# Bucket codes in one instruction per unit, spread by four transfers; a third query buffer; a token copy that is held back

## The chip, the cores and the metric

The kernel runs on one core of a Trainium2 chip. The time is that of the whole launch on the device, in microseconds (us). TensorE (PE) multiplies matrices into PSUM, VectorE (DVE), ScalarE (ACT) and GpSimd (POOL) work on tiles, and SyncE (SP) issues nearly all transfers. Each engine runs its own list of instructions in order, so one that waits holds up all that stand behind it.

## What is computed

The reference, cut to its core: attention in which a query sees only the keys of its own hash bucket, a feed-forward layer, and a layer with eight experts of which each token uses two.

```python
q_bits = (einsum('bhsd,dk->bhsk', q, proj) > 0)      # 6 bits; the same for k
mask = q_bucket[:, :, :, None] == k_bucket[:, :, None, :]
scores = where(mask, scale * q @ k.T, -1e9)
x = softmax(scores) @ v                              # batch 2, heads 8, 768 tokens, head 64
h = x @ w_in; x = (h * sigmoid(1.702 * h)) @ w_out   # 1536 tokens, 512 -> 2048 -> 512
top2 of noisy gate logits; out[t] += w * (relu(x[t] @ w1[e]) @ w2[e])   # 8 experts, 512 -> 1024 -> 512
```

## The kernel before

The attention runs in 96 steps, g = 0 to 95: a step is one head and 128 queries against all 768 keys. Sixteen steps make a chunk (256 queries, 8 heads); there are three chunks for each of the two batches. In a step PE multiplies queries by keys (`qk`, L227), DVE copies the scores out of PSUM and takes their maximum (`rowmax`, L239), ACT takes the exponential (L248), and the result is split in two halves of 16 bits, by ACT (L287) and by DVE (L294 or L296), and transposed by a DMA (`e_lo`, L300). PE then multiplies by the values (`pv`, L341). Chunk by chunk, some steps behind, the feed-forward layer runs in between (L433, L444), its result goes to the tile `xr`, and the router (`route`) picks two experts per token and scatters the rows to `slots` in DRAM (L658, issued by POOL). The expert layer (L772, L803) follows when all is scattered.

Queries and keys come in units. A query unit (24 of them) holds two heads of 256 queries, a key unit (16) one head of 768 keys. A unit is loaded (`load`, L124 or L128), split into 16-bit halves on ACT, DVE and POOL into a tile `qsa` or `ks` (`stack`), transposed by a DMA into `qt` or `kt` (`turn`, L160), one half of it copied once more by a DMA (`again`, L164), and projected by PE (`buckets`, L173). The projection of a unit is cut in four strips that lie in the PSUM tile `pb` at partitions 0, 32, 64 and 96, twelve rows each: six bits with both signs. `codes` (L181) compares each strip with zero and writes the twelve rows of codes, for that quarter of the tokens, into partitions 64 to 75 of `qt` or `kt`. They are extra rows of the contraction in `qk` (76 rows in its second half), where unequal bits add a penalty that no exponential survives. So `qk` of a step needs the codes of its query unit and its key units. `pb` has one buffer, which the router's small products use too.

Up to step 99 a scheduler decides the order of instructions when the kernel is built, from the order of the code, the dependencies and its own estimates; so any edit may move other work. From step 100 on the order is that of the code. The weights of the feed-forward layer, 64-bit floats, are decoded by DVE (L401, L404, L407) during the first two chunks.

The last two words of a row of `xr` hold the token's number: L612 copies it on DVE. It depends on nothing but a free buffer of `xr`, of which there are two.

Of the kernel before, what the change touches and what calls it, by code (L numbers as in the profile page):

```python
# [8 lines left out]
F16 = mybir.dt.float16  # L9
I32 = mybir.dt.int32  # L10
# [4 lines left out]
OP = mybir.AluOpType  # L15
# [3 lines left out]
DM = H * D  # L19
# [13 lines left out]
CT = 2  # L33
NCH = NT // CT
CQ = CT * 128
NBITS = 6
BIG = 65504.0
# [26 lines left out]
def fused(ctx: ExitStack, tc: tile.TileContext, q, k, v, proj, w_in, w_out, w_gate, w_noise, noise,  # L64
# [16 lines left out]
                            channel_multiplier=1)  # L81
    ident32 = consts.tile([128, 128], F32)
    nc.vector.tensor_copy(ident32, ident)
    pr = {nm: consts.tile([128, 3, 2 * NBITS], F16, name=f"p{nm}") for nm in "qk"}
    thr = consts.tile([128, 2], F32)
    for j in range(4):
        nc.gpsimd.iota(thr[j * 32:j * 32 + 32, 0:1], pattern=[[1, 1]], base=-NBITS, channel_multiplier=1,
# [4 lines left out]
    def proj_parts():  # L92
        p32 = rt.tile([128, NBITS], F32, name="p32", tag="zc", bufs=1)
        nc.sync.dma_start(p32[:64], proj)
        nc.sync.dma_start(p32[64:], proj)

        p3 = rt.tile([128, 3, NBITS], F16, name="p3", tag="z", bufs=1)
        nc.vector.tensor_scalar(p3[:, 0], p32, GP, GP, op0=OP.add, op1=OP.subtract)
        nc.vector.tensor_tensor(p32, p32, p3[:, 0], op=OP.subtract)
        nc.vector.tensor_copy(p3[:, 1], p32)  # L100
        nc.vector.tensor_tensor(p32, p32, p3[:, 1], op=OP.subtract)
        for nm, a0 in (("q", 0), ("k", 64)):
            w = pr[nm]
            h, l = slice(a0, a0 + 64), slice(64 - a0, 128 - a0)
            nc.vector.memset(w[l, 0], 0.0)
            for j in range(2):
                c, sg = slice(j * NBITS, (j + 1) * NBITS), SH if j == (nm == "k") else -SH
                nc.vector.tensor_scalar(w[h, 0:2, c], p3[h, 0:2], sg, 0.0, op0=OP.mult, op1=OP.add)
                nc.vector.tensor_scalar(w[h, 2, c], p32[h], sg, 0.0, op0=OP.mult, op1=OP.add)
                nc.vector.tensor_scalar(w[l, 1:3, c], p3[l, 0:2], sg, 0.0, op0=OP.mult, op1=OP.add)  # L110
# [2 lines left out]
    NU = B * NCH * 4 * HP  # L113


    raw, rows, kts, qts, vts, bks = {}, {}, {}, {}, {}, {}
    FL = "p h c d -> p (h c) d"


# [12 lines left out]
    def stack(nm, b, u):  # L132
        x = raw.pop((nm, b, u)).rearrange(FL)
        nh, n = (2, CT) if nm == "q" else (1, NT)
        if nm == "q":
            sa = att.tile([128, nh, n, 128], F16, name="qsa")
        else:
            sa = moe.tile([128, nh, n, 128], F16, name="ks", tag="wraw" if b else "gt", bufs=PARAM["NW"] if b else 4)
        rows[nm, b, u] = sa
        h0 = 0 if nm == "q" else 64  # L140
        hi, lo = (sa[:, :, :, c:c + 64].rearrange(FL) for c in (h0, 64 - h0))
        nc.scalar.activation(x, x, AF.Copy, scale=SH)
        eng = nc.gpsimd if PARAM["HE"](nm, b) == "P" else nc.vector
        eng.tensor_scalar(hi, x, GX, GX, op0=OP.add, op1=OP.subtract)
        nc.gpsimd.tensor_tensor(lo, x, hi, op=OP.subtract)

    def turn(nm, b, u):
        sa = rows.pop((nm, b, u))
        hp, i = u
        if nm == "q":  # L150
            xt = att.tile([128, 2, 2, CT, 128], F16, name="qt", bufs=3)
            qts[b, hp, i] = xt
        elif i == 0:
            xt = att.tile([128, 2, 2, NT, 128], F16, name="kt", bufs=4)
            kts[b, hp] = xt
        else:
            xt = kts[b, hp]
        dst = (xt if nm == "q" else xt[:, :, i:i + 1]).rearrange("p s h c t -> p s (h c) t")
        rows[nm, b, u] = dst
        nc.sync.dma_start_transpose(dst[:, 0], sa.rearrange("p h c d -> p (h c d)"))  # L160
# [5 lines left out]
    def buckets(nm, b, u):  # L166
        xt = rows[nm, b, u][:, 0].rearrange("p c t -> p (c t)")
        n = xt.shape[1] // 4
        pb = psr.tile([128, NT * 32], F32, name="pb", bufs=1)
        bks[nm, b, u] = pb  # L170
        for s in range(3):
            for j in range(4):
                nc.tensor.matmul(pb[j * 32:j * 32 + 2 * NBITS, :n], pr[nm][:, s], xt[:, j * n:j * n + n],  # L173
                                 start=(s == 0), stop=(s == 2))

    def codes(nm, b, u):
        xt, pb = rows.pop((nm, b, u))[64:KB, 1].rearrange("p c t -> p (c t)"), bks.pop((nm, b, u))
        n, sg = xt.shape[1] // 4, int(nm == "k")
        for j in range(4):
            sl = slice(j * 32, j * 32 + 2 * NBITS)  # L180
            nc.vector.tensor_scalar(xt[:, j * n:j * n + n], pb[sl, :n], thr[sl, sg:sg + 1], -BIG if sg else BIG,  # L181
                                    op0=OP.is_gt, op1=OP.mult)
            yield

    FU = PARAM["FU"]
    vfs = {}
# [351 lines left out]
    rst = {}  # L538
# [6 lines left out]
    def route(ci):  # L545
# [56 lines left out]
        for c in range(2):  # L602
# [2 lines left out]
            yield  # L605
        nc.vector.tensor_tensor(mk[:, ci], oh[:, :, 0], oh[:, :, 1], op=OP.add)
        yield
        nc.vector.tensor_tensor(cum[:, 1], cum[:, 0], mk[:, ci, 0], op=OP.add)
        yield

        me = mst[ci, "xr"][:, :, 2 * DM:].bitcast(F32)
        nc.vector.tensor_copy(mst[ci, "xr"][:, :, 2 * DM:2 * DM + 2].bitcast(I32),  # L612
                              tok[:, b, cc * CT:(cc + 1) * CT, None])
        yield
        nc.vector.tensor_copy(me[:, :, 1:2], ef[:, :, 0:1])
        yield
# [213 lines left out]
    def at(g, f, *a):  # L830
        todo.setdefault(g, []).append((f, a))
# [4 lines left out]
    def soon(g, f, *a):  # L836
        first.setdefault(g, []).append((f, a))
# [22 lines left out]
    def stacks(g, nm, b, u):  # L860
        oh = PARAM["OH"]
        at(g - 2, load, nm, b, u)
        at(g, stack, nm, b, u)
        soon(g + 1, turn, nm, b, u)
        start(g + PARAM['BK'], again, nm, b, u)
        start(g + PARAM['BK'], buckets, nm, b, u)
        at(g + oh, codes, nm, b, u)

    for b in range(B):
        for hp in range(HP):  # L870
# [70 lines left out]
    g_lo = min(todo)  # L941
    for g in range(g_lo, G1 + 1):
        if g == max(PARAM["GM"], g_lo):
            order.enter_context(tc.manual_schedule(engines={
                mybir.EngineType.PE, mybir.EngineType.DVE, mybir.EngineType.Activation,
                mybir.EngineType.Pool, mybir.EngineType.SP}))
        if g == NU + 3:
            att_ctx.close()
            m2 = ctx.enter_context(tc.tile_pool(name="m2", bufs=2))
        prev = steps.get(g - 1, [])  # L950
        if 0 <= g + 2 < NU:
            qk(g + 2)
        for f, a in early.pop(g, []):
            f(*a)
        for x in prev:
            moe_act(*x)
        if 0 <= g + 1 < NU:
            rowmax(g + 1)
            expo(g + 1)
            e_hi(g + 1)  # L960
        for f, a in first.pop(g, []):
            f(*a)
        for x in prev:
            moe_dve(*x)
        if 0 <= g < FU:
            e_turn(g)
            e_copy(g)
        elif FU <= g < NU:
            e_lo(g)
        for x in steps.get(g, []):  # L970
            moe_pe(*x)
        for x in prev:
            moe_split(*x)
        by_turns(todo.pop(g, []))
# [159 lines left out]
```

## Time and profile before

| what | value |
| --- | --- |
| median of 3 runs | 830.18 us (829.44 to 830.46) |
| the profiled execution, whole / span of its instructions | 828.85 / 827.0 us |
| busy: PE, DVE, ACT, POOL | 720.8, 545.6, 442.0, 273.8 us |
| mean granted clock of TensorE | 0.953 of full speed |
| L181, all 160 instructions | 59.98 us on DVE |

The page of the profile gives busy times and the costliest groups over the whole span. Since the stages have different limits, the views by stretch say more: the first chunk ends at about 94 us, the weights are decoded by about 200 us, the second batch begins at about 258 us, and from about 530 us on only the experts run.

### The profile page before, as it was taken

How to read it: one execution, taken by the hardware profiler on the slowest of the kernel's cores; microseconds unless marked ns; L12 is line 12 of the kernel's file. 1: busy time of each engine (PE TensorE's matmuls, PEld its weight loads, DVE VectorE, ACT ScalarE, POOL GpSimd, SP SyncE). 2: the span in 40 equal slices, each digit the busy share in tenths (PEclk: the TensorE clock that was granted, in tenths of full speed). 3: DMA queues.
4: the chain of work that ended last, by engine and by line, in shares of the span. 5: the costliest groups of instructions: out<-in, count | busy, mean ns of one | idle time of the engine just before them, and what ended most of it. 6: DMA issues, size and time to landing. Idle time of an engine off the chain costs nothing.

```text
span 827.0 us, 14864 instructions
## 1 busy us (share of the span) xinstructions
PE 720.8 (87%) x5494; PEld 431.2 (52%) x5495; DVE 545.6 (66%) x1279; ACT 442.0 (53%) x875; POOL 273.8 (33%) x302
## 2 busy tenths in 40 slices
PE   3767787878889788979999999896999999999994
PEld 1444355434654466547557658365545545555452
DVE  8998999988888679667867824563526435354220
ACT  3788676665676566557557715333524435344220
POOL 5446366634456123404222223221120311302112
PEclk9897699998999899999999999998999999999998
DMA  8985586999999996776587550657768768677313
GB/s 206 232 233 149 159 201 151 287 262 225 165 195 201 188 218 119 151 128 106 105 170 116 109 185 14 198 174 201 176 179 235 151 176 185 148 202 156 75 17 44
DMA packets 245340, 136.30 MB, mean 165 GB/s; under 512 B 200016, under 2 KB 221072, under 8 KB 245264
## 3 DMA queue, kind: packets, MB, share of 16 engines
q1 hardware_dynamic: 239248, 122.16, 62.6%
q0 software_dynamic: 6016, 13.16, 8.6%
q8 instruction: 44, 0.72, 0.4%
q14 instruction: 32, 0.26, 0.1%
HBM read 61.48 MB, written 23.20 MB: 102 GB/s over the span
## 4 chain that ended last, share of the span: by engine, by line
PE 46%; DVE 21%; DMA 12%; issue 8%; ACT 5%; POOL 4%; SPq 2%; POOLq 0%; DVEq 0%; ACTq 0%
PE ph L772 15%; PE py L803 14%; PE h L433 6%; PE px L444 5%; DVE e L239 4%; DVE er L296 4%; DMA slots<-xr,si 3%; PE s L227 2%; DMA et<-er 2%; ACT er L287 2%; POOL slots L658 2%; DVE wraw L407 2%; DVE wf L404 2%; DVE qt L181 2%; DMA k<-in_k_dram 2%
## 5 line engine op out<-in xcount | busy, mean ns | idle before, releaser
L772 PE MATMUL ph<-xg,ew 128*128 128x400 f16 (+2 forms) x864 | 136.3, 321 | 10.8 <-DMA xg<-slots 9.9
L444 PE MATMUL px<-wo,gt 128*128 128x512 f16 x576 | 139.1, 392 | 6.9 <-ACT wo L418 4.6
L433 PE MATMUL h<-xt,wi 128*128 128x256 f16 x1152 | 137.2, 275 | 7.3 <-DVE xr L467 3.9
L716 DVE SCALAR_TENSOR_TENSOR ew<-w,ew 128x1024 f16<-128x1024 f32 x64 | 77.9, 1225 | 86.6 <-ACT ew L715 86.6
L433 PEld LDWEIGHTS <-wi 128*128 128x128 f16 x1152 | 111.3, 98 | 28.9 <-issue 10.8
L803 PE MATMUL py<-ew,ht 128*128 128x512 f16 x576 | 125.8, 379 | 0.0
L820 POOL DMA_INDIRECT out_dram<-yo,ti x32 | 50.1, 1564 | 211.2 <-ACT yo L813 201.8
L772 PEld LDWEIGHTS <-ew 128*128 128x128 f16 x864 | 83.4, 101 | 62.1 <-issue 8.1
L227 PE MATMUL s<-kt,qt 76*128 76x256 f16 (+3 forms) x384 | 87.5, 353 | 27.5 <-DVE e L239 24.6
L478 POOL TENSOR_TENSOR gt<-th,gt 128x512 f16<-128x512 f32 x48 | 61.7, 1286 | 113.9 <-ACT gt L477 112.8
L444 PEld LDWEIGHTS <-gt 128*128 128x128 f16 x576 | 56.2, 100 | 75.5 <-issue 17.5
L239 DVE TENSOR_SCALAR_CACHE_REDUCE e<-s 128x768 f32<-128x768 f32 x96 | 90.9, 951 | 5.3 <-PE pt L266 3.9
L296 DVE SCALAR_TENSOR_TENSOR er<-e,mx,er 128x768 f16<-128x768 f32 x68 | 73.5, 1084 | 28.1 <-ACT er L287 27.3
L803 PEld LDWEIGHTS <-ht 128*128 128x128 f16 x576 | 56.2, 98 | 67.1
L248 ACT ACTIVATE e<-e,mx 128x768 f32<-128x768 f32 x96 | 89.3, 930 | 1.8
L287 ACT ACTIVATE er<-e,mx 128x768 f16<-128x768 f32 x68 | 63.1, 931 | 29.2 <-DMA et<-er 16.2
L782 ACT ACTIVATE ht<-ph 128x400 f16<-128x400 f32 (+2 forms) x72 | 33.6, 467 | 69.2 <-PE ph L772 68.9
L715 ACT ACTIVATE ew<-w 128x1024 f16<-128x1024 f32 x64 | 66.4, 1049 | 6.4 <-DMA w<-in_moe_w_dram 6.3
L227 PEld LDWEIGHTS <-qt 76*128 76x128 f16 (+1 forms) x384 | 36.6, 103 | 60.5 <-issue 30.0
L813 ACT ACTIVATE yo<-py,wv 128x512 f32<-128x512 f32 x24 | 16.5, 687 | 87.8 <-PE py L803 51.0
L783 DVE SCALAR_TENSOR_TENSOR ht<-ph,ht 128x400 f16<-128x400 f32 (+2 forms) x72 | 37.5, 524 | 33.9 <-ACT ht L782 33.8
L247 ACT ACTIVATE mx<-mx 128x1 f32<-128x1 f32 x96 | 18.9, 197 | 64.1 <-DVE e L239 63.8
(182 smaller groups left out, 923.9 us busy)
## 6 DMA issues: line engine op xcount, KB each, us to landing
w<-in_moe_w_dram SPq DMA_DIRECT2D x64, 512.0 KB, 4.9
wraw<-in_moe_w_in_dram SPq DMA_DIRECT2D x16, 512.0 KB, 5.3
wraw<-in_moe_w_out_dram SPq DMA_DIRECT2D x16, 512.0 KB, 4.8
slots<-blank SPq DMA_DIRECT2D x6, 1032.0 KB
v<-in_v_dram SPq DMA_DIRECT2D x24, 192.0 KB, 3.0
out_dram<-zeros SPq DMA_DIRECT2D x13, 256.0 KB, 3.4
k<-in_k_dram SPq DMA_DIRECT2D x16, 192.0 KB, 4.4
q<-in_q_dram SPq DMA_DIRECT2D x24, 128.0 KB, 2.9
```

The source lines that it names most:

```text
L227: nc.tensor.matmul(ps[:, n0 * 128:n1 * 128], qt[:kr, s, h, t, :], kt[:kr, s, h, n0:n1, :].rearrange("p c t -> p (c t)"), start=(s == 0), s ...
L239: nc.vector.tensor_scalar(e32, st[g]["ps"][:, :S], -FAR, -TOP, op0=OP.max, op1=OP.max, accum_out=mx[:, 0:1])
L248: nc.scalar.activation(e32, e32, AF.Exp, scale=SS, bias=st[g]["mx"][:, 1:2], accum_out=sms[b, cc, hp][:, 2 * h + t:2 * h + t + 1] if g < N ...
L287: nc.scalar.activation(er[:, 0], st[g]["e"], AF.Copy, scale=r)
L296: nc.vector.scalar_tensor_tensor(er[:, 1], d["e"], d["mx"][:, 3:4], er[:, 0], op0=OP.mult, op1=OP.subtract)
L433: nc.tensor.matmul(ph[:, a, :], wi[ws][:, d, f0:f0 + 128], xt[:, d, xs, :], start=(d == 0 and ws == 0 and xs == 0), stop=(d == HP - 1 and ...
L444: nc.tensor.matmul(px, gts[ci, f // 2][:, gs, f % 2, t * 128:t * 128 + 128], wo[ws][:, f, :], start=(f == 0 and gs == 0 and ws == 0), stop ...
L478: nc.gpsimd.tensor_tensor(gt[:, 1], th, gt[:, 0], op=OP.subtract)
L715: nc.scalar.activation(hi, x, AF.Copy, scale=SW1 if j == 0 else SW2)
L716: nc.vector.scalar_tensor_tensor(lo, x, SW1 if j == 0 else SW2, hi, op0=OP.mult, op1=OP.subtract)
L772: nc.tensor.matmul(ph[:, :c1 - c0], w[:, ws, d * FE + f * 128:d * FE + f * 128 + 128], xg[e, p][:, xs * HP + d, :], start=(d == 0 and ws = ...
L803: nc.tensor.matmul(py, ht[:, f, hs, t * 128:t * 128 + 128], w[:, ws, f * DM:(f + 1) * DM], start=(i == 0), stop=(i == n - 1))
```

## The change

`pr`, the weights of the projection, get 32 columns instead of 12, zeros in the other 20, so that the four strips fill all 128 partitions of `pb`. `codes` compares all of them in one DVE instruction and writes into the unit's `qsa` or `ks` tile, which has been transposed by then. A new step, `spread`, at the start of the next step, moves the four strips to their rows of `qt` or `kt` by four transfers of SP. The `qsa` or `ks` tile is held until these have read it, and `qsa` gets three buffers instead of two. L612 (L617 after) is tied to stand behind the running sum of `route` (`cum`) in DVE's list, as long as the scheduler orders.

```diff
-    pr = {nm: consts.tile([128, 3, 2 * NBITS], F16, name=f"p{nm}") for nm in "qk"}
+    pr = {nm: consts.tile([128, 3, 32], F16, name=f"p{nm}") for nm in "qk"}
...
-            nc.vector.memset(w[l, 0], 0.0)
+            nc.vector.memset(w, 0.0)
...
-            sa = att.tile([128, nh, n, 128], F16, name="qsa")
+            sa = att.tile([128, nh, n, 128], F16, name="qsa", bufs=3)
...
-                nc.tensor.matmul(pb[j * 32:j * 32 + 2 * NBITS, :n], pr[nm][:, s], xt[:, j * n:j * n + n],
+                nc.tensor.matmul(pb[j * 32:j * 32 + 32, :n], pr[nm][:, s], xt[:, j * n:j * n + n],
...
     def codes(nm, b, u):
-        xt, pb = rows.pop((nm, b, u))[64:KB, 1].rearrange("p c t -> p (c t)"), bks.pop((nm, b, u))
+        xt, pb = rows[nm, b, u][64:KB, 1].rearrange("p c t -> p (c t)"), bks.pop((nm, b, u))
         n, sg = xt.shape[1] // 4, int(nm == "k")
+        cd = sas.pop((nm, b, u)).rearrange("p h c d -> p (h c d)")
+        nc.vector.tensor_scalar(cd[:, :n], pb[:, :n], thr[:, sg:sg + 1], -BIG if sg else BIG, op0=OP.is_gt, op1=OP.mult)
+        bks[nm, b, u] = cd
+
+    def spread(nm, b, u):
+        xt, cd = rows.pop((nm, b, u))[64:KB, 1].rearrange("p c t -> p (c t)"), bks.pop((nm, b, u))
+        n = xt.shape[1] // 4
         for j in range(4):
-            sl = slice(j * 32, j * 32 + 2 * NBITS)
-            nc.vector.tensor_scalar(xt[:, j * n:j * n + n], pb[sl, :n], thr[sl, sg:sg + 1], -BIG if sg else BIG,
-                                    op0=OP.is_gt, op1=OP.mult)
-            yield
+            nc.sync.dma_start(xt[:, j * n:j * n + n], cd[j * 32:j * 32 + 2 * NBITS, :n])
...
-        nc.vector.tensor_tensor(cum[:, 1], cum[:, 0], mk[:, ci, 0], op=OP.add)
+        behind = nc.vector.tensor_tensor(cum[:, 1], cum[:, 0], mk[:, ci, 0], op=OP.add)
...
-        nc.vector.tensor_copy(mst[ci, "xr"][:, :, 2 * DM:2 * DM + 2].bitcast(I32),
-                              tok[:, b, cc * CT:(cc + 1) * CT, None])
+        with ExitStack() if rst.get("set") else tc.issue_after(behind.ins):
+            nc.vector.tensor_copy(mst[ci, "xr"][:, :, 2 * DM:2 * DM + 2].bitcast(I32),
+                                  tok[:, b, cc * CT:(cc + 1) * CT, None])
...
         at(g + oh, codes, nm, b, u)
+        soon(g + oh + 1, spread, nm, b, u)
```

What this does to the lists of instructions shows at three places. The first is SP's list at the start of the program (`ks_155` and `qsa_159` are the first key and query unit; `kt`, `qt` their transposed tiles). Before:

```order
L164 DMA kt_163<-kt_163 64x768
L164 DMA qt_165<-qt_165 64x512
L160 DMA_TRANSPOSE kt_163<-ks_211 128x6x128
L390 DMA wraw_225<-in_moe_w_in_dram 128x1024
L124 DMA q32_231<-in_q_dram 128x2x128
L160 DMA_TRANSPOSE kt_233<-ks_227 128x6x128
L164 DMA kt_163<-kt_163 64x768
```

and after:

```order
L164 DMA kt_163<-kt_163 64x768
L164 DMA qt_165<-qt_165 64x512
L187 DMA kt_163<-ks_155 12x192 x4
L187 DMA qt_165<-qsa_159 12x128 x4
L160 DMA_TRANSPOSE kt_163<-ks_213 128x6x128
L394 DMA wraw_227<-in_moe_w_in_dram 128x1024
L124 DMA q32_233<-in_q_dram 128x2x128
L160 DMA_TRANSPOSE kt_235<-ks_229 128x6x128
L164 DMA kt_163<-kt_163 64x768
```

Eight transfers of codes now stand ahead of the next key unit's transposition, and they wait for DVE. From here to the first transposition of a softmax (L300 before, L304 after) SP has 91 transfers before and 133 after: 56 for codes, and 14 others fewer (loads that now come later).

The second place is DVE's list where the copy of the token numbers stands in the second batch's first chunk (`xr_4372` is the third chunk's tile, `er` a step's low half, `xr_2178` the first chunk's). Before:

```order
L467 SCALAR_TENSOR_TENSOR xr_3242<-px_2998,xr_3242 128x512
L296 SCALAR_TENSOR_TENSOR er_3204<-e32_3198,mx_3197,er_3204 128x768
L252 TENSOR_SCALAR mx_3244<-mx_3244 128x1
L239 TENSOR_SCALAR e32_3296,mx_3295<-s_3237 128x768
L253 RECIPROCAL mx_3244<-mx_3244 128x1
L612 COPY xr_4372<-tok_107 128x2
L296 SCALAR_TENSOR_TENSOR er_3251<-e32_3245,mx_3244,er_3251 128x768
```

and the first such copy of the changed kernel (its first chunk; in the kernel before this one stood among the first ten instructions of the program):

```order
L610 TENSOR_TENSOR mk_122<-oh_2923 128x16
L180 TENSOR_SCALAR ks_2650<-pb_2857,thr_87 128x192
L635 RECIPROCAL xr_2178<-d1_2930 128x2
L612 TENSOR_TENSOR cum_123<-cum_123,mk_122 128x8
L617 COPY xr_2178<-tok_107 128x2
L637 TENSOR_TENSOR xr_2178<-xr_2178,d1_2930 128x2
```

The copy has moved from a place some chunks ahead of its own chunk's routing to one inside it.

The third place is SP's list where the second batch's first key units are prepared, between the transpositions of softmax steps. Before:

```order
L164 DMA kt_2929<-kt_2929 64x768
L300 DMA_TRANSPOSE et_2687<-er_2593 128x12x128
L160 DMA_TRANSPOSE qt_2859<-qsa_2814 128x4x128
L160 DMA_TRANSPOSE kt_3057<-ks_3013 128x6x128
L164 DMA qt_2859<-qt_2859 64x512
L300 DMA_TRANSPOSE et_2687<-er_2681 128x12x128
```

and after:

```order
L304 DMA_TRANSPOSE et_2707<-er_2613 128x12x128
L128 DMA k32_2738<-in_k_dram 128x384
L187 DMA kt_2560<-ks_2513 12x192 x4
L187 DMA qt_2562<-qsa_2519 12x128 x4
L304 DMA_TRANSPOSE et_2707<-er_2701 128x12x128
```

Between the two transpositions of a pair of steps stand transfers of codes, which wait for DVE and for nothing else.

## Rows read from the trace of the kernel before

**Rows 1.** Busy us of each engine by stretch of the span, with granted clock and DMA share.
```profile
core 0: us, PE busy (x) PEld busy (x) DVE busy (x) ACT busy (x) POOL busy (x), PEclk, DMA share, GB/s
0.00:94.00 94.00, 57.43 (x443) 32.23 (x444) 83.46 (x198) 63.80 (x151) 48.85 (x86) 0.87 0.78 199
94.00:201.00 107.00, 84.59 (x617) 49.25 (x618) 101.31 (x175) 71.06 (x142) 59.51 (x46) 0.90 0.88 223
201.00:336.00 135.00, 117.79 (x1081) 77.91 (x1081) 111.22 (x296) 87.51 (x194) 53.50 (x49) 0.95 0.91 177
...
365.00:530.00 165.00, 159.94 (x1342) 107.67 (x1340) 112.10 (x309) 97.28 (x196) 46.34 (x44) 1.00 0.60 126
530.00:827.00 297.00, 275.42 (x1859) 151.13 (x1857) 119.83 (x257) 109.03 (x167) 58.62 (x73) 0.97 0.61 151
```

**Rows 2.** L239 by the same stretches: DVE busy, and two instructions for each step.
```profile
0.00:94.00 94.00, 15.25 (x32) 0.87 0.78 199
94.00:201.00 107.00, 19.11 (x40) 0.90 0.88 223
201.00:336.00 135.00, 26.92 (x56) 0.95 0.91 177
```

**Rows 3.** Chain of work that ended last, 336 to 365 us, shares by line.
```profile
by line: DMA slots<-xr,si 28.3%; DMA qt<-qsa 14.8%; issue 13.7%; POOL slots L658 12.2%; DVE er L296 9.6%; DMA q<-in_q_dram 7.2%; DVE e L239 3.8%; POOL qsa L144 3.7%; ACT e L248 3.2%; POOL qsa L145 2.7%; ACT q L142 1.4%; DVE ps__4236 L638 1.
```

**Rows 4.** DVE around L612, in order of time; in brackets the idle time before.
```profile
272.49 0.17 DVE L612 COPY xr<-tok 128x2 int32<-128x2 int32 x1 [6.02 <-DMA slots<-xr,si]
...
351.57 0.17 DVE L612 COPY xr<-tok 128x2 int32<-128x2 int32 x1 [5.91 <-DMA slots<-xr,si]
```

**Rows 5.** PE at the same two places.
```profile
269.78 0.63 PE L341 MATMUL pv<-et,vt 128*64 128x256 f16 x8
275.60 0.66 PE L173 MATMUL pb<-kt,pk 128*12 128x192 f16 x12 [5.19 <-DVE kt L181]
...
355.36 0.81 PE L227 MATMUL s<-kt,qt 128*128 128x512 f16 x4 [3.38 <-DVE e L239]
```

**Rows 6.** L181 over the whole span: duration least, median, most, first and last start.
```profile
L181 DVE TENSOR_SCALAR qt<-pb,thr x96: 342/346/359, 14.6 to 447.5; 12x128 f16<-12x128 f32 x96
L181 DVE TENSOR_SCALAR kt<-pb,thr x64: 407/414/425, 10.9 to 301.2; 12x192 f16<-12x192 f32 x64
```

**Rows 7.** L181 by stretch: DVE busy and instructions, four to a unit.
```profile
0.00:94.00 94.00, 23.03 (x60) 0.87 0.78 199
94.00:201.00 107.00, 5.57 (x16) 0.90 0.88 223
201.00:336.00 135.00, 23.02 (x60) 0.95 0.91 177
```

**Rows 8.** Issue time on SP of small transfers (the four of L739) and of transpositions.
```profile
L739 SPq DMA_DIRECT2D mt<-slots x32: 408/418/482, 563.7 to 762.7; - x32
...
L300 SPq DMA_TRANSPOSE et<-er x80: 1275/1488/6345, 100.0 to 476.2; - x80
```

**Rows 9.** SP's own waits, 0 to 94 us: first and last of 18 (total, times, longest).
```profile
SPq L128 <- POOL vt L209: 7.9, 7, 2.8
...
SPq L128 <- ACT mx L247: 0.2, 1, 0.2
```

**Rows 10.** SP's own waits, 201 to 336 us: first and last of 22.
```profile
SPq L300 <- DVE mx L253: 8.1, 5, 4.2
...
SPq L128 <- POOL vt L209: 0.5, 1, 0.5
```

**Rows 11.** Transfers by line: size, median us from issue to landing.
```profile
kt<-kt SPq DMA_DIRECT2D x16, 96.0 KB, 3.5
...
mt<-slots SPq DMA_DIRECT2D x32, 0.2 KB, 1.8
```

**Rows 12.** What PE and its weight loads waited for, whole span: total, times, longest.
```profile
PE pb L173 <- DVE kt L181: 11.0, 6, 5.2
...
PEld L227 <- DVE qt L181: 4.2, 7, 2.1
```

## What I predicted, before the changed kernel had run

> **What bounds the kernel now.** I read the table by stretch first [rows 1], because the kernel has three different limits. Up to 94 us DVE is busy for 83.5 of 94 us, and from 94 to 201 us for 101.3 of 107: these 201 us hold 36 steps [rows 2] and DVE sets their pace. From 201 to 336 us it is busy for 111.2 of 135 while PE has 117.8, and the transfer engines are at 0.91: nothing is full, and what ends there is a chain of waits. From 365 to 530 us PE has 159.9 of 165, and from 530 us on 275.4 of 297; there nothing that DVE or SP gains can be seen. So an edit pays only by bringing the point at about 365 us forward, where PE has become the limit, and it can pay at most what PE idles before that.
>
> The second view was the chain of waits from 336 to 365 us [rows 3]: 28.3% of it are the scatter transfers to `slots` and another 12.2% POOL issuing them. That is odd, since nobody reads `slots` before the experts. The DVE timeline tells why [rows 4]: twice L612, a copy of a few words, waits 6.02 and 5.91 us for the scatter, because the scheduler put it ahead of time, where its buffer of `xr` is still being read. All of DVE's list stands behind it, and PE runs dry in turn: 5.19 us the first time, 3.38 us the second [rows 5].
>
> Third, SP: its own waits add up to 41.0 us in 0 to 94 (18 rows) and 48.5 us in 201 to 336 (22 rows) [rows 9, 10]. So it issues for about 53 of 94 and 86 of 135 us.
>
> **The change part by part.**
>
> *The held copy (a).* It stands behind its own chunk's sum now, long after the old buffer's scatter. Both stalls should go. DVE gets 11.9 us back [rows 4], but the end only moves by what PE lost, 5.19 + 3.38 = 8.6 us [rows 5]. Ends: 0, if another wait stands at the same place (the next late thing is `er`'s transposition, which SP issues), and 12. I take -8.6, since PE is the limit right behind it.
>
> *Fewer instructions on DVE.* A key unit takes 4 x 0.414 us now and one such instruction after, a query unit 4 x 0.346 [rows 6]: the length is set by the columns, which stay, so I take the same 0.414 and 0.346 for 128 partitions. Saved are 1.24 and 1.04 us a unit, 16 x 1.24 + 24 x 1.04 = 44.8 us in all. By stretch [rows 7]: 15 units (8 keys, 7 queries) in 0 to 94 us, 17.2 us; 4 query units in 94 to 201, 4.2 us; 15 units again in 201 to 336, 17.2 us; the rest lies where PE is the limit and is worth 0.
>
> *Four transfers for it, on SP.* The nearest rows are the four small transfers that the expert stage issues in a row, 0.418 us each [rows 8]; 1.7 us a unit. In 0 to 94 us that is 56 x 0.42 = 23.5 us, less 14 loads that now come later (at about the same 0.42, 5.9 us): 53 + 17.6 = 71 of 94 us. In 201 to 336 it is 60 x 0.42 = 25 us: 86 + 25 = 111 of 135. So SP goes from 56% to 75% and from 64% to 83% at the old pace, and would be at 90% if the pace rose by a tenth. Behind a transfer of codes, which waits for DVE, stand loads and the transpositions of softmax steps (1.49 us each [rows 8]), and behind those POOL, PE and the next units. So the gain of each stretch is cut:
>
> - (b) 0 to 94 us: of 17.2 us I take -3. The first units' transpositions stand behind eight transfers of codes (8 x 0.42 = 3.4 us later, and so on for each unit), so the first steps come later and DVE decodes weights meanwhile; that work is not lost, which is why I expect a small gain and not a loss. Ends -12 (SP never late) and +8 (half of the 17.6 us shows).
> - (c) 94 to 201 us: DVE at 95%, SP with few units; -3.5 of 4.2. Ends -6 (also what was decoded ahead) and 0.
> - (d) 201 to 336 us: neither engine is full. -1; ends -10 and +12 (half of the 25 us).
>
> *The way from projection to query (f).* Before, the codes are in place when the fourth instruction ends. After: one instruction, four issues (1.7 us), and a landing, 1.8 us for 0.2 KB and 3.5 us for 96 KB [rows 11]; the transfers of codes have 3 to 4.6 KB, so I take 2.2 us, nearer to the small one. That is 0.41 + 1.7 + 2.2 = 4.3 instead of 1.7 us, 2.6 us later. A step takes 107/20 = 5.4 us [rows 2], and most units are prepared several steps ahead, so it is hidden under other steps except where `qk` already waits for codes: 7 times in the weight loads' row [rows 12]. Two or three of these at 2.6 us give +6. Ends 0 and +12.
>
> *The projection's buffer (g).* PE waits 11.0 us for L181 to empty `pb`, of which 5.2 are the stall counted in (a) [rows 12]. The other 5.8 us shrink with one instruction for four: I take -2.5; ends -5 and 0.
>
> *The rest.* 32 columns of weights instead of 12: the products have the same 128 or 192 columns of moving data, and the loads of weights run beside them; 0, with an end of +3. A third `qsa` buffer pays for the tile being held longer; no price of its own.
>
> Here a rule speaks against the change. The row shows that 0.2 KB need 1.8 us to land, where 96 KB need 3.5 [rows 11]: a small transfer is nearly all overhead. The Trainium skill says so too (DMA: Bandwidth & Descriptors, Rules for kernel authors): many small transfers should be one large one, since below 64 KB one pays mostly overhead. By that rule 160 transfers of under 5 KB should lose against 120 DVE instructions; what it would do here is rival 1, worked out from rows there.
>
> **Sum.** -8.6 (a) - 3 (b) - 3.5 (c) - 1 (d) + 6 (f) - 2.5 (g) = -12.6 us against the profiled execution's 828.85: 816.25. The median of the runs lies 1.33 us higher, so 817.6 us.
>
> **The rivals.**
>
> 1. *SP takes DVE's place (slower).* Transfers of codes wait in an in-order list, and everything behind them is late. For it: SP at 83% in 201 to 336 us before any gain of pace, and SP already waits 8.1 us for L253 there [rows 10], so it does get blocked by DVE. Against it: 48.5 us of waits to spare. It decides when the transfers of codes are late by more than what SP waits now. Price: +8 (b), +12 (d), +8 (f), with (a) -8.6 and (c) -3 kept, (g) 0: +16.4, giving 828.85 + 16.4 + 1.33 = 846.6 at its full size; at half of (b) and (d), +6.4, 836.6. I give 837 as its time.
> 2. *DVE's time is worth nearly all of its price.* For it: DVE at 89 and 95% in the first 201 us. (a) -8.6, (b) -9, (c) -4, (d) -8, (f) +4, (g) -3 = -28.6, giving 801.6.
> 3. *The gains and the costs cancel.* The stall at L612 goes, but another wait ends at the same time, as the transpositions are behind codes in SP's list: (a) -2, (b) and (c) -3, (d) 0, (f) +4, (g) 0 = -1, giving 829.2. This is also the case in which the copy moves but the change doesn't do what it says.
>
> **How the numbers follow.** The forecast has 0.44 with a range of its own from 808 to 826; rival 1 has 0.25, rival 2 0.15, rival 3 0.16. About 0.2% (1.7 us) is what a measurement of this kernel can tell from no change. Rival 3 is spread over all three signs: 0.10 same, 0.04 faster, 0.02 slower. The forecast puts all on faster but 0.01 on same. So faster 0.43 + 0.15 + 0.04 = 0.62, same 0.11, slower 0.27. For the range I leave out the lower third of rival 2 (some 0.07) and the upper half of rival 1 (some 0.12): 799 to 838.
>
> **What would show it.** (a): no L612 (L617 now) with an idle time above 1 us before it, and no PE gap of 3 to 5 us behind the scatters. (b), (c): the 17th L239 at 88 to 93 us, which comes after 94 us now, and the 37th some 5 to 9 us ahead of 201 us [rows 2]. (d): the 65th 10 to 17 us ahead of 336 us if I am right, at or behind it if rival 1 rules; then the wait views name the transfers of codes in front of `qk`, and SP's waits on L180. (f): `qk` waits on transfers of codes of some 2 to 3 us each, fewer than eight of them. From 365 us to the end the stages should have their old lengths. I am wrong if the first 201 us take no less time although DVE's busy share there falls by ten points or more, or if a stall of PE stands in a place that none of these rows shows.

## The result: slower by 0.9%, and the profile after

The changed kernel takes 836.94 us (median; 836.42 to 838.05), the kernel before 829.92 us beside it: the ratio is 1.0086, 95% interval 1.0069 to 1.0104. The profiled execution spans 835.6 us against 827.0. So the sign of the forecast was wrong, and the case that came is rival 1, SP in DVE's place, close to the time given for it.

The busy times by stretch of the changed kernel, in the columns of [rows 1], answer those rows:

```profile
0.00:94.00 94.00, 53.47 (x380) 29.50 (x382) 62.67 (x142) 51.98 (x117) 42.21 (x75) 0.78 0.64 166
94.00:201.00 107.00, 85.41 (x693) 53.48 (x692) 95.88 (x165) 78.73 (x167) 59.32 (x51) 0.90 0.90 235
201.00:336.00 135.00, 117.96 (x1031) 76.43 (x1031) 84.86 (x234) 82.34 (x174) 46.58 (x46) 0.96 0.68 143
336.00:365.00 29.00, 18.32 (x148) 9.70 (x147) 14.66 (x42) 14.98 (x33) 10.10 (x10) 0.91 0.77 190
365.00:530.00 165.00, 155.60 (x1323) 106.17 (x1323) 107.38 (x292) 102.42 (x211) 46.38 (x43) 0.96 0.66 142
530.00:835.60 305.60, 287.72 (x1923) 156.72 (x1921) 132.39 (x287) 115.71 (x177) 67.16 (x79) 0.98 0.64 157
```

One row of before from the same view, which [rows 1] left out:

```profile
336.00:365.00 29.00, 25.62 (x159) 13.03 (x158) 17.69 (x48) 13.36 (x27) 6.97 (x7) 0.94 0.80 145
```

DVE's busy share fell from 89% to 67% in the first stretch and from 82% to 63% in the third, and the transfer engines went from 0.78 to 0.64 and from 0.91 to 0.68. Everything is less busy, and the time is longer: the limit is something that these columns don't count. PE's column gives the loss. Up to 530 us PE has been busy for 430.8 us, where it had been for 445.4 before: -4.0, +0.8, +0.2, -7.3 and -4.3 us by stretch, 14.6 us in all. From 530 us on it idles 17.9 us instead of 21.6, and its busy time over the whole span is 2.3 us shorter (718.5 for 720.8). 14.6 - 3.7 - 2.3 = 8.6 us, which is the difference of the spans.

The column that is missing is SP's. In the first view below SP issues what stands in its list at the start and at 322 us, "x4" being four in a row; the second gives the issue times (least, median, most, in ns) of L187, the transfers of codes, over the whole span.

```profile
start us, us, engine line op out<-in xcount [idle before <-releaser]
...
11.07 3.23 SPq L187 DMA_DIRECT2D kt<-ks  x4
14.63 3.00 SPq L187 DMA_DIRECT2D qt<-qsa  x4
17.73 1.25 SPq L160 DMA_TRANSPOSE kt<-ks  x1
...
322.02 6.24 SPq L187 DMA_DIRECT2D kt<-ks  x8
328.37 1.42 SPq L304 DMA_TRANSPOSE et<-er  x1
```

```profile
L187 SPq DMA_DIRECT2D qt<-qsa x96: 713/724/1706, 14.6 to 462.9; - x96
L187 SPq DMA_DIRECT2D kt<-ks x64: 713/724/1722, 11.1 to 327.5; - x64
```

One transfer of codes occupies SP for 0.724 us, not for the 0.418 us of [rows 8]: 160 x 0.724 = 115.8 us instead of 66.9. The second key unit's transposition starts at 17.73 us, where SP had issued it at 10.90 us before:

```profile
10.90 1.34 SPq L160 DMA_TRANSPOSE kt<-ks  x1
```

At 322 us a softmax step's transposition waits behind 6.24 us of codes.

The steps follow. L243 (L239 before), two instructions to a step, answers [rows 2]:

```profile
0.00:94.00 94.00, 13.00 (x28) 0.78 0.64 166
94.00:201.00 107.00, 20.69 (x43) 0.90 0.90 235
201.00:336.00 135.00, 23.36 (x50) 0.96 0.68 143
```

These are 14, 21.5 and 25 steps instead of 16, 20 and 28. The fifth step (g = 4) shows in DVE's timeline at 52.63 us, where it stood at 36.42, and the 65th at 359.45 instead of 336.69. Before:

```profile
36.42 0.96 DVE L239 TENSOR_SCALAR_CACHE_REDUCE e<-s 128x768 f32<-128x768 f32 x1
...
336.69 0.95 DVE L239 TENSOR_SCALAR_CACHE_REDUCE e<-s 128x768 f32<-128x768 f32 x1
```

and after:

```profile
52.63 0.94 DVE L243 TENSOR_SCALAR_CACHE_REDUCE e<-s 128x768 f32<-128x768 f32 x1
...
359.45 0.96 DVE L243 TENSOR_SCALAR_CACHE_REDUCE e<-s 128x768 f32<-128x768 f32 x1
```

In the first 365 us PE's waits for transfers that SP issues have grown, while its wait for the maximum of the scores (L239, L243 after) has hardly changed (total, times, longest). Before:

```profile
PE s L227 <- DVE e L239: 22.1, 19, 3.4
...
PE pb L173 <- DMA kt<-ks: 9.1, 1, 9.1
```

and after:

```profile
PE pb L173 <- DMA kt<-ks: 22.3, 5, 9.2
...
PE s L231 <- DVE e L243: 20.2, 12, 6.2
...
PE s L231 <- DMA qt<-qsa: 11.0, 5, 4.8
...
PE pb L173 <- DMA qt<-qsa: 7.4, 5, 2.9
...
PE s L231 <- DMA kt<-ks: 3.6, 3, 2.7
...
PE pb L173 <- DVE ks L180: 0.6, 1, 0.6
```

At `pb` (L173) the transfers waited for are the units' transpositions, at `s` (L231) those of codes. The last row answers the 11.0 us of [rows 12]: for DVE to empty `pb` PE hardly waits any more.

### The profile page after: what moved, and what is told of

The parts are those of the page before. It is cut to its first block, busy times and chain, and to the rows that moved or that the text cites. A ratio compares the mean times of both kernels' runs of the same rounds, so it can differ in the third digit from the quotient of the medians.

```text
span 835.6 us, 14985 instructions
## 1 busy us (share of the span) xinstructions
PE 718.5 (86%) x5494; PEld 432.0 (52%) x5495; DVE 497.8 (60%) x1159; ACT 446.2 (53%) x875; POOL 271.7 (33%) x302
## 5 line engine op out<-in xcount | busy, mean ns | idle before, releaser
L437 PE MATMUL h<-xt,wi 128*128 128x256 f16 x1152 | 140.4, 277 | 9.7 <-DVE th L467 5.4
L448 PE MATMUL px<-wo,gt 128*128 128x512 f16 x576 | 131.8, 383 | 2.4 <-DVE th L467 2.4
L231 PE MATMUL s<-kt,qt 128*128 128x512 f16 (+3 forms) x384 | 90.1, 356 | 38.9 <-DVE e L243 23.9
L825 POOL DMA_INDIRECT out_dram<-yo,ti x32 | 54.0, 1687 | 203.8 <-ACT yo L818 196.8
L300 DVE SCALAR_TENSOR_TENSOR er<-e,mx,er 128x768 f16<-128x768 f32 x68 | 71.5, 1054 | 55.9 <-ACT er L291 55.8
L482 POOL TENSOR_TENSOR gt<-th,gt 128x512 f16<-128x512 f32 x48 | 57.8, 1204 | 134.0 <-ACT gt L481 131.7
L243 DVE TENSOR_SCALAR_CACHE_REDUCE e<-s 128x768 f32<-128x768 f32 x96 | 90.8, 950 | 5.1 <-PE s L231 2.8
L808 PEld LDWEIGHTS <-ht 128*128 128x128 f16 x576 | 56.4, 98 | 66.9
L231 PEld LDWEIGHTS <-qt 128*128 128x128 f16 (+1 forms) x384 | 34.7, 102 | 75.5 <-issue 27.4
L345 PE MATMUL pv<-et,vt 128*64 128x256 f16 x720 | 53.0, 288 | 7.5 <-DMA et<-er 7.4
```

The source lines that it names most:

```text
L231: nc.tensor.matmul(ps[:, n0 * 128:n1 * 128], qt[:kr, s, h, t, :], kt[:kr, s, h, n0:n1, :].rearrange("p c t -> p (c t)"), start=(s == 0), s ...
L243: nc.vector.tensor_scalar(e32, st[g]["ps"][:, :S], -FAR, -TOP, op0=OP.max, op1=OP.max, accum_out=mx[:, 0:1])
L300: nc.vector.scalar_tensor_tensor(er[:, 1], d["e"], d["mx"][:, 3:4], er[:, 0], op0=OP.mult, op1=OP.subtract)
L437: nc.tensor.matmul(ph[:, a, :], wi[ws][:, d, f0:f0 + 128], xt[:, d, xs, :], start=(d == 0 and ws == 0 and xs == 0), stop=(d == HP - 1 and ...
L448: nc.tensor.matmul(px, gts[ci, f // 2][:, gs, f % 2, t * 128:t * 128 + 128], wo[ws][:, f, :], start=(f == 0 and gs == 0 and ws == 0), stop ...
L482: nc.gpsimd.tensor_tensor(gt[:, 1], th, gt[:, 0], op=OP.subtract)
```

## The experiments

My theory after the result: the change does give DVE's time back, and that is worth a lot, but 160 transfers on SP cost more. The rivals: DVE's time is worth nothing here and the codes simply arrive late on their longer way; or the held copy, the third buffer or the order that the scheduler finds makes the difference. The scheduler may reorder with every edit; so each result is read with its own traces, and the last run puts DVE's time back into the fastest kernel and leaves everything else in its code. How far the order moved can be read from DVE's list in the traces (how many instructions two lists have in common in the same order). In four pairs all but four or fewer keep their order: the kernel before and the held copy alone; the changed kernel with and without the held copy; the changed kernel with 12 and with 16 rows a transfer; the two kernels with the old way at the start and ACT's queue, with 12 and with 16 rows. In the other pairs an eighth to a quarter of DVE's instructions stand elsewhere, and there an effect of the order isn't excluded. Ratios are to the kernel before on the same chip.

**The held copy alone.**

```diff
-        nc.vector.tensor_tensor(cum[:, 1], cum[:, 0], mk[:, ci, 0], op=OP.add)
+        behind = nc.vector.tensor_tensor(cum[:, 1], cum[:, 0], mk[:, ci, 0], op=OP.add)
...
+        with ExitStack() if rst.get("set") else tc.issue_after(behind.ins):
```

> The kernel before with the held token copy alone (codes by DVE in four instructions, two query buffers). In the kernel before the copy stalled DVE twice, 6.02 and 5.91 us, and PE 5.19 and 3.38 us behind it. If these stalls were the path to the end: 829.9 - 8.6 = 821 us, range 817 to 825. If another wait stands at the same place: 828 to 831. Either way no idle time above 1 us in front of the copy.

Measured: 825.95 us, ratio 0.994 (0.9916 to 0.9964), about -5.0 us of 830, between the two ranges expected. No copy of a token number has an idle time before it, so both stalls of [rows 4] are gone, but in the third stretch PE is busy no longer than before (115.61 us for 117.79), and 28 steps lie there as before. Another wait stands at the same places: between 262 and 290 us DVE now waits 7.7 us for ACT's half of the softmax result (L287) instead of 1.8, between 336 and 365 us 5.5 instead of 2.6.

**The changed kernel without the held copy** (the same edit undone).

> The changed kernel with the token copy free again. If the held copy is worth in the changed kernel what its stalls cost in the kernel before: 836.9 + 6 to 9 us, 843 to 846. If SP is late anyway and DVE has time to spare, the stall costs nothing: 836 to 839.

Measured: 839.74 us, just between the two ranges expected, ratio 1.0104 (1.0061 to 1.0147) where the whole change has 1.0086. That is 1.5 us by the ratios, and the intervals overlap; the stalls have come back, though smaller:

```profile
DVE xr L616 <- DMA slots<-xr,si: 5.7, 2, 3.4
```

So the copy is worth 5 us in the kernel before and, in the changed one, nothing that could be told from zero; it isn't what lost.

**The transfers' cost without their use.** The kernel before with the held copy; codes are made the old way, on DVE, and SP issues four transfers per unit at the place where `spread` would stand. They read the codes and write a tile that nobody reads, so nobody waits for them to land.

```diff
...
+    def dummy(nm, b, u):
+        xt = cds.pop((nm, b, u))
+        n = xt.shape[1] // 4
+        to = rt.tile([128, 192], F16, name="dumd", bufs=2)
+        for j in range(4):
+            nc.sync.dma_start(to[j * 32:j * 32 + 2 * NBITS, :n], xt[:, j * n:j * n + n])
...
+        soon(g + oh + 1, dummy, nm, b, u)
```

> The kernel before with the held copy, and four further transfers of twelve rows a unit that SP issues where the changed kernel issues its codes: they read the codes after DVE has written them, and nobody waits for what they write. Theory 1 (SP's issue time alone does it: 160 x 0.72 = 115 us more on SP, and loads and transpositions behind them late): slower than the held copy alone by 15 us or more, and slower than the kernel before; the fifth step later than 45 us. Theory 2 (the longer way from projection to query does it, issue time is hidden): within 3 us of the held copy alone, the fifth step at 36 to 40 us.

Measured: 864.05 us, ratio 1.0401 (1.0361 to 1.0441), 38.1 us above the held copy alone on the same chip. The issue times and the steps by stretch (L249):

```profile
L183 SPq DMA_DIRECT2D dumd<-qt x96: 713/725/1384, 14.8 to 484.1; - x96
...
L183 SPq DMA_DIRECT2D dumd<-kt x64: 713/736/1445, 11.2 to 337.9; - x64
```

```profile
0.00:94.00 94.00, 15.07 (x32) 0.80 0.61 163
...
201.00:336.00 135.00, 22.67 (x48) 0.92 0.69 147
```

No wait in the trace is for the landing of these transfers, and the loss is larger than that of the whole change. So SP's list alone can cost that much: the time to issue, and what stands behind it while it waits for codes. The fifth step comes at 44.5 us, a little before the 45 us expected; some two thirds of the loss arise later, between the 37th and the 65th step (159.8 us for 134.3 with the held copy alone). The run also prices the other side, if cost and gain simply add, which the changed order doesn't promise. The whole change stands 1.0086 - 0.994 = 1.5% (12 us) above the held copy, the transfers alone 38 us: the rest of the change, DVE's relief above all, would then have given back some 26 us.

**All transfers issued by ACT.**

```diff
-            nc.sync.dma_start(xt[:, j * n:j * n + n], cd[j * 32:j * 32 + 2 * NBITS, :n])
+            nc.scalar.dma_start(xt[:, j * n:j * n + n], cd[j * 32:j * 32 + 2 * NBITS, :n])
```

> The changed kernel with the 160 transfers of codes issued by ACT instead of SP. ACT is busy for 53%, DVE no longer the limit. Theory 1 (SP's issue time): SP gets 115 us back and the first steps come early again (fifth step before 42 us); ACT gets some 0.7 us for each transfer, 44 us in the first 94 us, so the time lands between 815 and 830. Theory 2 (the way from projection to query): that way is as long as before, 833 to 840.

Measured: 823.06 us, ratio 0.9897 (0.9855 to 0.9939). The transfers take ACT as long as SP, 0.736 us each. Steps by stretch (L243):

```profile
0.00:94.00 94.00, 12.40 (x26) 0.87 0.77 196
...
201.00:336.00 135.00, 29.62 (x62) 0.94 0.88 187
```

The time lies in the range of theory 1, but its sign at the start failed: the fifth step comes at 45.5 us and not before 42. In the first stretch it is worse than the changed kernel (13 steps for 14): now ACT's own work stands behind the codes, and there ACT waits 18.8 us and POOL 11.7 us for transfers of codes. In the third it does 31 steps where the kernel before does 28. The place of the loss moves with the queue.

**Shorter issue, the same waits.** The strips of `pb` have 32 rows, of which 12 count. A transfer that takes 16 rows (or 32) writes rows that nobody reads.

```diff
-        xt, cd = rows.pop((nm, b, u))[64:KB, 1].rearrange("p c t -> p (c t)"), bks.pop((nm, b, u))
+        xt, cd = rows.pop((nm, b, u))[64:64 + 16, 1].rearrange("p c t -> p (c t)"), bks.pop((nm, b, u))
...
-            nc.sync.dma_start(xt[:, j * n:j * n + n], cd[j * 32:j * 32 + 2 * NBITS, :n])
+            nc.sync.dma_start(xt[:, j * n:j * n + n], cd[j * 32:j * 32 + 16, :n])
```

> The changed kernel with 16 rows in each transfer of codes instead of 12 (four rows of padding go along; nobody reads them). Its issue on SP took 0.72 us with 12 rows, 0.418 us for the four 16-row transfers of the expert stage. If the row count sets it: about 0.42 us, 48 us less on SP, and the time falls by 8 us or more, to 820 to 829. If it is something else about these transfers: 0.72 us and 836 to 838.

> The same with 32 rows. If the issue grows with the rows: 0.8 us or more and slower than the changed kernel (840 or more). If a count that 16 divides is what helps: about 0.45 us, as with 16 rows, 820 to 829. If neither: 0.72 us, 836 to 838.

Measured: 16 rows 827.89 us, ratio 0.9951 (0.992 to 0.9981); 32 rows 832.69 us, 1.0018 (0.9995 to 1.0041). With 16 rows the issue takes

```profile
L187 SPq DMA_DIRECT2D qt<-qsa x96: 507/587/1401, 14.7 to 449.1; - x96
L187 SPq DMA_DIRECT2D kt<-ks x64: 507/587/2150, 11.1 to 317.3; - x64
```

so 160 x 0.137 = 21.9 us less on SP, and the kernel is 1.35% (11 us) faster than with 12 rows: the time is in the first range, though the issue takes neither 0.42 nor 0.72 us. This is the cleanest pair: all but 3 of DVE's 1164 instructions keep their order, and in the trace's records of packets those of a key unit's codes, where they can be told from others, end as soon after the fourth issue as before (median 0.78 us with 12 rows, 0.82 with 16). What is left to differ is the time to issue, and taking a fifth of it away made the slower kernel a faster one: half of what SP saved shows in the time. With 32 rows the issue takes the same 0.588 us, but the kernel is some 5 us slower than with 16, in none of the ranges expected; there only a quarter of the saving shows. Why stays open: 8 and 12 KB instead of 4 and 6 move, and 154 of DVE's instructions stand elsewhere.

**The old way at the start, the new one after it.** The first 15 units (eight keys, seven queries), which are prepared in the first 94 us, get their codes as before; the other 25 as in the change.

```diff
+    def old(nm, b, u):
+        return (nm == "k" and b == 0) or (nm == "q" and b == 0 and (u[1] == 0 or u[1] == 1 and u[0] < 3))
...
+        if old(nm, b, u):
...
+            for j in range(4):
+                sl = slice(j * 32, j * 32 + 2 * NBITS)
+                nc.vector.tensor_scalar(xo[:, j * no:j * no + no], po[sl, :no], thr[sl, so:so + 1], -BIG if so else BIG,
+                                        op0=OP.is_gt, op1=OP.mult)
...
+            return
```

> The changed kernel, with the codes of the first 15 units (8 keys, 7 queries) made as before by four DVE instructions; the other 25 units spread by SP. Theory 1 (SP's issue time, wherever SP is dense): the first 94 us are as in the kernel before (fifth step at 36 to 37 us, 17th at 93 to 96), but between the 37th and the 61st step it loses 10 to 18 us again as the changed kernel did; 827 to 834. Theory 3 (the late start alone made the change slow, the rest is only its echo): 816 to 823.

Measured: 831.42 us, ratio 1.0007 (0.9984 to 1.003). Steps by stretch (L259):

```profile
0.00:94.00 94.00, 15.32 (x32) 0.78 0.81 201
94.00:201.00 107.00, 20.00 (x42) 0.88 0.87 221
201.00:336.00 135.00, 23.98 (x50) 0.99 0.72 148
```

The start is that of the kernel before, and the first 201 us now hold one step more; the third stretch loses three of its 28 steps again. The 61st step comes 129 us after the 37th, where the kernel before takes 116: the loss of 10 to 18 us that theory 1 expected. So there are two places of loss, and each is where units are prepared on SP.

**The same, with the 25 units' transfers issued by ACT** (`nc.scalar` in `spread`, as above).

> The same, with the other 25 units' transfers issued by ACT. If SP's load is all that is wrong with the transfers: first 94 us as in the kernel before, no loss between the 37th and the 61st step, 814 to 821, faster than the transfers on ACT for all units (823). If ACT's own list is now the limit: 821 to 826.

Measured: 802.33 us, ratio 0.9643 (0.9611 to 0.9675). That is faster than either range expected. With ACT in SP's place the third stretch holds 31 steps, and PE's busy time there rises from 117.8 to 127.5 us. Busy times in that stretch:

```profile
201.00:336.00 135.00, 127.49 (x1169) 82.34 (x1167) 105.70 (x282) 95.63 (x209) 53.67 (x49) 1.00 0.88 189
```

**The same with 16 rows a transfer.**

> As the mixed kernel whose first 15 units spread their codes the old way and whose other 25 units use four transfers issued by ScalarE (802.33 us), but each transfer carries 16 rows instead of 12 (the added rows are never read). 25 x 4 transfers at 0.14 to 0.15 us less issue time each take some 14 us from ScalarE. If ScalarE's issue time is what still ends waits in steps 36 to 64: 796 to 800 us. If ScalarE is not the limit: 801 to 804 us. If the wider rows cost in landing time: above 804 us.

Measured: 797.68 us, ratio 0.9636 (0.9606 to 0.9666). The issue on ACT takes 0.53 us now, but the interval covers that of the run before it: the gain of the shorter issue isn't told apart here. Its median is the lowest of this study. Its third stretch:

```profile
201.00:336.00 135.00, 130.78 (x1190) 84.30 (x1188) 108.46 (x283) 95.91 (x209) 53.79 (x49) 1.00 0.94 194
```

**Is it the third buffer?** The held copy and `bufs=3` for `qsa`, nothing else.

> The kernel before with two parts of the change only: the held copy of the token rows and the third buffer of the query rows (qsa); codes and their spreading stay as in the kernel before (four instructions a unit on VectorE). The held copy alone gave 825.95 us. If the third buffer gives nothing by itself: 823 to 829 us. If the third buffer is what brings the mixed kernel with its transfers on ScalarE's queue to 802 us: below 815 us.

Measured: 825.61 us, ratio 0.9948 (0.9922 to 0.9973), as the held copy alone. The buffer gives nothing by itself, and the order changed here too (161 of DVE's 1284 instructions stand elsewhere) without an effect on the time that can be seen.

**Is it DVE's time?** The fastest kernel, with DVE's old work put back as dead instructions.

```diff
+        for j in range(3):
+            sl = slice(j * 32, j * 32 + 2 * NBITS)
+            nc.vector.tensor_scalar(cd[sl, n:2 * n], pb[sl, :n], thr[sl, sg:sg + 1], -BIG if sg else BIG,
+                                    op0=OP.is_gt, op1=OP.mult)
```

> The mixed kernel with 16-row transfers issued by ScalarE (797.68 us), plus three dead VectorE instructions behind each of the 25 single ones: the old comparison of a 12-row strip, written to columns that nobody reads. They put back 8 x 1.24 + 17 x 1.04 = 27.6 us of VectorE's time and nothing else; the result is unchanged. If VectorE's relief is what made the gain of the mixed kernel over the held copy alone (826 us): 815 to 828 us. If the gain comes from the order that the scheduler finds, or from the third buffer: 796 to 806 us.

Measured: 824.43 us, ratio 0.9938 (0.9912 to 0.9965), the time of the held copy alone. The dead instructions and the third stretch:

```profile
L196 DVE TENSOR_SCALAR qsa<-pb,thr x51: 320/344/348, 110.3 to 442.2; 12x128 f16<-12x128 f32 x51
L196 DVE TENSOR_SCALAR ks<-pb,thr x24: 396/410/415, 223.0 to 294.3; 12x192 f16<-12x192 f32 x24
```

```profile
201.00:336.00 135.00, 123.23 (x1113) 80.35 (x1112) 115.65 (x306) 87.70 (x192) 50.65 (x48) 0.97 0.83 173
```

51 x 0.344 + 24 x 0.410 = 27.4 us of DVE put back, and (0.9938 - 0.9636) x 830 = 25 us lost. PE is busy 7.6 us less in the third stretch, at a granted clock of 0.97 of full speed for 1.00. Transfers, third buffer and held copy are the same in both, so they don't make the gain by themselves: the dead instructions undo all that stood above the held copy alone. Two things came with them. They keep `pb` busy longer, as the old ones did; PE waits 1.6 us for that and its weight loads 2.4. And the order changed: of the other 1209 instructions of DVE 981 keep theirs. So it is likely, and not shown by itself, that the gain is DVE's time. For it speaks that 26 and 25 us come from kernels of different order, and that the third buffer's new order cost nothing.

## Why the prediction was wrong

The expected range of the time held (838 at its upper end), but the sign did not, and the size of the loss agrees with rival 1's 837 us partly by luck: rival 1 took the same too small price and halved its effect, where the transfers alone cost 38 us and, if the two add, some 26 us came back.

- **The price of an issue: wrong, the step that failed.** I took 0.418 us from the small transfers of the expert stage [rows 8] as the nearest row; the transfers of codes take 0.724 us. That those read DRAM and these another tile isn't the reason: the kernel before had tile-to-tile transfers too, of 64 rows, and they took 0.47 to 0.52 us.

```profile
L164 SPq DMA_DIRECT2D qt<-qt x24: 461/518/1351, 10.3 to 427.5; - x24
L164 SPq DMA_DIRECT2D kt<-kt x16: 461/473/1216, 9.7 to 276.8; - x16
```

  What the runs show is the number of rows: 12 take 0.724 us, 16 and 32 take 0.587. I gave no upper end for this price at all, although the transposition in the same group takes 1.488 us; the ends of (b) and (d) were cut from the too small sum. An estimate of what the price alone did: 160 x 0.306 = 49 us too little on SP, of which a quarter to a half shows by the runs with 32 and 16 rows, is 13 to 25 us; the changed kernel's 837 us less that is 812 to 824, around the 817.6 forecast.
- **SP's room, read over the whole stretch: wrong too.** "41.0 us of waits in 94" [rows 9] is an average. Between the first step and the fifth, 17.06 to 36.42 us, SP's own waits add up to 4.9 us (5 rows) in the kernel before.

```profile
SPq L160 <- POOL ks L145: 1.6, 1, 1.6
SPq L160 <- POOL wi L419: 1.4, 2, 1.0
SPq L164 <- DMA kt<-ks: 1.2, 1, 1.2
SPq L160 <- POOL qsa L145: 0.5, 1, 0.5
SPq L128 <- ACT mx L247: 0.2, 1, 0.2
```

  In the changed kernel SP starts 16 transfers of codes in this piece, 11.8 us in all, and it takes 35.3 us instead of 19.4. Even by 0.418 us they would have needed 6.7 us where 4.9 were free. The waits that made up the 41 us lie mostly later: 17 us of the 41 are waits at L128 and L390, loads that stand there until another engine has freed a tile.
- **(b) -3: wrong sign.** Step 16, the 17th, comes at 101.32 us instead of 94.66, +6.7, near the end of +8. **(c) -3.5: nearly nothing.** The next 20 steps take 107.6 us for 107.1; DVE's busy share fell from 95% to 90% and no step came sooner. The sign that I had named for being wrong, that the first 201 us take no less time although DVE's share falls by ten points, applied: the 37th step comes at 208.93 us instead of 201.75, and DVE's share of the 201 us fell from 92% to 79%.
- **(d) -1: wrong sign.** Steps 36 to 64 (from the start of the 37th to that of the 65th) take 150.5 us instead of 134.9, +15.6 and beyond the end of +12, although the first stall of (a) and part of (g) lie in there as gains.
- **(a) -8.6: over-sized.** The stalls of L612 went as foreseen, but alone the copy gives 5.0 us (3.0 to 7.0), and within the changed kernel 1.5 us that its measurement can't tell from nothing. The reason is the one that I had given for the lower end: with the copy alone, DVE waits at the same places for ACT's half of a result instead (7.7 us for 1.8, 5.5 for 2.6), and PE doesn't get all of its gap back.
- **(f) +6: the count was wrong.** PE's queue waits eight times for transfers of codes, 14.6 us in all, where I had said fewer than eight. But the experiment in which nobody waits for the landing lost more, and with the old way at the start the same four transfers gave 802 us on ACT's queue where they gave 831 on SP's; so the way itself isn't the main cause. How these 14.6 us divide between late issue and landing isn't shown.
- **(g) -2.5: the wait went as foreseen, and further.** 11.0 us of waiting for DVE to empty `pb` became 0.6. But PE's waits at the same instruction for transpositions rose to 29.7 us (22.3 and 7.4) from 10.3, so PE gained nothing at that place. One instruction costs what each of the four did, as taken:

```profile
L180 DVE TENSOR_SCALAR qsa<-pb,thr x24: 336/346/352, 14.3 to 460.2; 128x128 f16<-128x128 f32 x24
L180 DVE TENSOR_SCALAR ks<-pb,thr x16: 404/414/419, 10.6 to 319.3; 128x192 f16<-128x192 f32 x16
```

- **Rival 2's reason was probably right as well.** In the kernels on ACT's queue DVE's time seems worth nearly its price: 25 of 27.4 us by the dead instructions, with the order as an open end. For the whole change it is less, some 26 us by the dummy transfers, where L181 and L180 took 59.98 and 14.91 us of DVE. I had let the first 201 us, where DVE's busy share was highest, carry most of it. No run shows what it is worth in the first 94 us, since the 802 us kernel keeps the old way there. Of the 25 us by which its profiled execution is shorter, 14 come between the 37th and the 65th step, where DVE had been busy for 82%, and 9 between the 65th and the 96th, a stretch in which I had expected nothing. So a busy share below 90% was no sign that DVE's time was free.
- **After step 64 a part comes back.** The 65th step is 22.8 us late, the 96th 13.7, the end 8.6: by 336 us PE had been busy only 3.0 us less than before, since 5.6 us more of the feed-forward layer had been done in place of the late steps.

The rule that I had set against the change, from the Trainium skill (DMA: Bandwidth & Descriptors, Rules for kernel authors), that many small transfers are mostly overhead, is borne out here: 160 transfers of 3.0 and 4.5 KB cost 38 us of the kernel's time when nothing used them. What was short was the issuing queue and not the transfer engines, whose share in the third stretch fell from 0.91 to 0.68 in the changed kernel.

## What to carry to other kernels

Where work moves from an engine to a queue, add its issue time to the queue's list over the shortest piece in which the next steps depend on it, not over a stage: 41 us of free time in a stage were 4.9 us where it counted. No row of the kernel before gives the price of a 12-row issue, not even its other tile-to-tile transfers (0.52 us at most by the median); so where the form of a transfer is new, carry the dearest row as an end of the range. And when a change loses, price its gain and its cost apart, by adding each alone: here some 26 us of gain seem to have lain under 38 us of cost, and another queue with room in that stage, with the old way kept at the start, gave a kernel of about 800 us.

## What was not expected of the hardware

- The issue time of a tile-to-tile transfer depends on its rows in an odd way: 12 rows (3.0 and 4.5 KB) take 0.724 us on SP, 16 and 32 rows (4 to 12 KB) 0.587, and the 64 rows of L164 in the kernel before 0.47 to 0.52. So four more rows make the issue shorter, and 16 more rows after that change nothing.
- On ACT's queue they are the same kind of load: 0.736 us with 12 rows, 0.53 with 16, and ACT's own instructions stand behind them.
- The landing, a median of 2.8 us for 4.0 and 6.0 KB (16 rows, ACT's queue, the 798 us kernel), lies between the two rows that had bounded it [rows 11]:

```profile
qt<-qsa ACTq DMA_DIRECT2D x68, 4.0 KB, 2.8
kt<-ks ACTq DMA_DIRECT2D x32, 6.0 KB, 2.8
```
